# One kilobyte a partition of a weight load sent as a transfer whose source has an outer dimension of 4

## The chip, the cores and the metric

The kernel runs on one core of a Trainium2 chip. The metric is the device time of one execution in microseconds; the median of three runs is 216.96 us (216.91 to 217.72). One execution was taken with the hardware profiler, and all rows shown are from that one. Its data comes from HBM through 16 DMA engines, which work side by side. A transfer is cut into packets, each a contiguous run of bytes, and the packets are shared out among the engines; a transfer has landed when the last engine that carries a part of it is done.

## The reference

A decode step for two sequences: a layer norm of one token each, a window attention over the last 4096 cached positions, a gated MLP, and the product of both added to the input.

```python
def _A_ref(x, k_cache, v_cache, wq, wo):
    B, Sq, D = x.shape                       # 2, 1, 512
    Hq, Dh = 32, 128
    Hkv, Sk = k_cache.shape[1], k_cache.shape[2]   # 8, 32768
    W = min(4096, max(256, Sk // 4))         # 4096
    rep = Hq // Hkv
    q = (x @ wq).reshape(B, Sq, Hq, Dh).transpose(0, 2, 1, 3)
    k = jnp.repeat(k_cache[:, :, Sk - W:, :], rep, axis=1)
    v = jnp.repeat(v_cache[:, :, Sk - W:, :], rep, axis=1)
    scores = jnp.einsum("bhqd,bhkd->bhqk", q, k) * (Dh ** -0.5)
    p = _softmax(scores, axis=-1)
    o = jnp.einsum("bhqk,bhkd->bhqd", p, v)
    return o.transpose(0, 2, 1, 3).reshape(B, Sq, Hq * Dh) @ wo

def _B_ref(x, w_in, w_sp, b_sp, w_out):
    z = _gelu(x @ w_in)                      # F = 1792, Fh = 896
    z1, z2 = z[..., :Fh], _layernorm(z[..., Fh:], axis=-1)
    g = jnp.einsum("ts,bsf->btf", w_sp, z2) + b_sp[None, :, None]
    return (z1 * g) @ w_out

xn = _layernorm(A_x)
return A_x + _A_ref(xn, ...) * _silu(_B_ref(xn, ...))
```

## The kernel before

All is float32. The input is 89.4 MB, nearly all of it the two caches' windows (16 loads of 4 MB, named k and v in the profile), wq (8 MB), wo (8 MB), w_in (3.5 MB) and w_out (1.75 MB). Every large load is issued on SP's queue, in program order, and each is spread over all 128 partitions.

**Buffers.** `slot` gives out 4 buffers of 32 KB a partition, in turn: w_in, wq rows for k = 0 and 1, wq rows for k = 2 and 3, K0, K1, V0, K2, V1 and so on. A load into a buffer is issued once the work that reads the buffer's earlier content is done. So K1 waits for the w_in products, V0 for the first half of wq, K2 for the second half, and later loads for the transposes (K) or the products (V) of the unit three loads back.

**wq.** Its row number is 4p + k (p the partition, k = 0 to 3), so a partition holds four neighbouring rows of 16 KB. The first two come in one transfer of 4 MB (line 130, a = 0), the other two in one transfer of 2 MB each (a = 2). `queries(k)` (lines 262 to 269) multiplies row group k: 8 products of 32 columns of `xnT[:, k, :]` (the normed input, transposed, with its 512 elements split in the same way) with 512 columns of wq, summed over k in two PSUM banks `pq`. The profile names them `q_ps`; each shows as two MATMUL entries. Between them lie the norm of the MLP's second half and, behind them, `y` (w_out), the copies `qs`, the transposes `qx`, the masked copies `xm`, the product `qa`, and `place_queries` (line 337), which fills `qb`.

**xnT.** Lines 193 to 198: the normed input `xn` is transposed by four TensorE transposes (one for each k) into PSUM and copied to `xnT`, whose unused columns were cleared.

**Attention.** Eight units of two heads each run through a hand-written order (the table ORDER, lines 27 to 52): transposes of K on VectorE (`T`, tile kts), shares and scores on TensorE, the softmax on ScalarE, products with V (`pv`, tile acc).

**The end.** wo comes in 4 MB, then pieces of 2, 1, 0.5, 0.25 and 0.25 MB (`load_wo`, lines 511 to 518), the last ones so that the last products (`Z`, tile so) have little left to do when the last bytes land. After `Z:3` come two VectorE operations (`res`) and the store.

**Small loads.** Line 139 loads x into `x4` with a source of outer dimension 4 (`by_group`, line 138: 4 x 2 x 128 elements), on ScalarE's queue, beside the first large load.

Of the kernel before, what the change touches and what calls it, by code (L numbers as in the profile page):

```python
# [9 lines left out]
F32 = mybir.dt.float32  # L10
# [4 lines left out]
P = 128  # L15
HQ, DH = 32, 128
# [4 lines left out]
def free_ap(t, offset, dims):  # L21

    return bass.AP(tensor=t.tensor, offset=t.offset + offset, ap=[list(t.ap[0])] + [list(d) for d in dims])
# [47 lines left out]
def kernel(  # L71
# [14 lines left out]
    pe, dve, act, sp = (InOrder(tc, e) for e in (nc.tensor, nc.vector, nc.scalar, nc.sync))  # L86
    B, _, D = x.shape
# [7 lines left out]
    KT = D // P  # L95
# [3 lines left out]
    DC = D // G  # L99
    SCALE = DH ** -0.5  # L100
    OFF = 30000.0 / SCALE

    fit = ctx.enter_context(tc.tile_pool(name="fit", bufs=1))
    fit.tile([P, 480], F32, tag="fit", name="fit")
# [2 lines left out]
    cst = ctx.enter_context(tc.tile_pool(name="cst", bufs=1))  # L107
# [3 lines left out]
    def slot(name, *shape):  # L111
        return ring.tile([P, *shape], F32, tag="slot", name=name)

    def bank(name, *shape):
        return ps.tile([P, *shape], F32, tag="kt", name=name, bufs=2)
# [9 lines left out]
    wq_v = wq.rearrange("(p k) f -> p k f", p=P)  # L125
    wqt = []
    for a in range(0, KT, 2):
        t = slot(f"wq{a}", 2, HQ * DH)
        for k, n in ((0, 2),) if a == 0 else ((0, 1), (1, 1)):
            sp.dma_start(t[:, k : k + n], wq_v[:, a + k : a + k + n, :])  # L130
        wqt += [t[:, 0], t[:, 1]]

    wb1 = cst.tile([1, 2], F32, tag="wb1", name="wb1")
# [21 lines left out]
    ident = cst.tile([P, P], F32, tag="ident", name="ident")  # L155
    make_identity(nc, ident)
    selw = cst.tile([P, 60], F32, tag="selw", name="selw")
    nc.gpsimd.memset(selw, 0.0)
    xnT = cst.tile([P, KT, 32], F32, tag="xnT", name="xnT")
    nc.gpsimd.memset(xnT, 0.0)  # L160
    ones = cst.tile([P, P], F32, tag="ones", name="ones")
    nc.gpsimd.memset(ones, 1.0)
# [29 lines left out]
    rsqrt(rs, va, "x")  # L192
    xn = sb.tile([B, D], F32, tag="o", name="xn", bufs=1)
    dve.tensor_scalar(xn, xs, mv[:, 0:1], rs, op0=ALU.subtract, op1=ALU.mult)
    pt = bank("xnT_ps", KT, B)
    for k in range(KT):
        pe.transpose(pt[:, k, :], xn.rearrange("b (p k) -> b k p", k=KT)[:, k, :], ident[:B, :B])
    dve.tensor_copy(xnT[:, :, :B], pt)

    same = cst.tile([P, G, 32], F32, tag="same", name="same")  # L200
# [15 lines left out]
    dve.tensor_reduce(other, free_ap(rowm, 0, [[4, 2], [8, REP]]), axis=AX.X, op=ALU.add)  # L216
    dve.tensor_scalar(other, other, -OFF, OFF, op0=ALU.mult, op1=ALU.add)
    diag = cst.tile([P, 4], F32, tag="diag", name="diag")
# [18 lines left out]
    for n in range(G):  # L237
        pz = bank(f"z{n}", 512)[:, :FC]
        for k in range(KT):
            pe.matmul(  # L240
                pz[32 * k : 32 * k + 32, :], xnT[:, k, :], win[:, k, n * FC : (n + 1) * FC],
                start=True, stop=True,
# [9 lines left out]
    pt = bank("zT_ps", 2, FT, B)  # L252
# [7 lines left out]
    pq = [ps.tile([P, 512], F32, tag=f"s{r}", name=f"q_ps{r}") for r in range(NR)]  # L260

    def queries(k):
        for r in range(NR):
            for g in range(G):
                c = (r * G + g) * 512
                pe.matmul(
                    pq[r][32 * g : 32 * g + 32, :], xnT[:, k, :], wqt[k][:, c : c + 512],
                    start=(k == 0), stop=(k == KT - 1),
                )

    queries(0)
    zT = cst.tile([P, 2, FT, B], F32, tag="zT", name="zT")
    dve.tensor_copy(zT, pt)
# [19 lines left out]
    per_b = [[0, FT], [1, B]]  # L293
    mean_over_rows(mean, z2, "mean_ps")
    queries(1)
    dve.tensor_scalar_mul(mean, mean, 1.0 / FH)
    dve.tensor_sub(z2, z2, free_ap(mean, 0, per_b))
# [5 lines left out]
    dve.tensor_scalar(z2, z2, wb[:, 0:1], wb[:, 1:2], op0=ALU.mult, op1=ALU.add)  # L303
    dve.tensor_mul(hT[:, :, 0 : 16 * B : 16], z1, z2)
    queries(2)
    queries(3)

# [4 lines left out]
    for j in range(FT):  # L312
        for g in range(G):
            pe.matmul(
                y[32 * g : 32 * g + 32, :], hT[:, j, :], wout[:, j, g * DC : (g + 1) * DC],
                start=(j == 0), stop=(j == FT - 1),
# [277 lines left out]
    for u in range(NU):  # L594
        p = Unit()
        p.u, p.m, p.kt, p.sh, p.ss, p.s, p.p, p.pT = u, None, {}, {}, {}, {}, {}, {}
        units.append(p)
    for line in ORDER.strip().split("\n"):
        for name in line.split():
            name, at = name.split(":")  # L600
            u, _, a = at.partition(".")
# [34 lines left out]
```

## Time and profile before

| what | value |
|---|---|
| median of 3 runs | 216.96 us (216.91 to 217.72) |
| profiled execution: its own time | 217.3 us |
| profiled execution: span, first to last instruction | 215.4 us |
| TensorE busy, share of the span | 65% |
| VectorE busy | 58% |
| ScalarE busy | 24% |
| read from HBM | 89.40 MB, 415 GB/s over the span |

An engine's share of busy time is an average over the whole span. The DMA row of the page counts how busy the 16 DMA engines are on average, so a share of 0.50 can mean that eight of them are busy and eight are done. Instruction rows give start, duration and, in brackets, how long the engine stood idle before and what released it. DMA rows on SPq are the issuing of a transfer, not its movement.

### The profile page before, as it was taken

The page shows a single profiled execution, that of the slowest core. Times are in us where ns is not written, and L with a number is a line of the kernel's source. Part 1 is how long each engine was busy: PE and PEld are TensorE (multiplying, and loading weights), DVE is VectorE, ACT ScalarE, POOL GpSimd, SP SyncE. Part 2 cuts the span into 40 slices and gives each one's busy share as a digit, 9 for nine tenths or more (in the row PEclk, how much of TensorE's full clock was granted, in tenths as well). Part 3 has the DMA queues.
Part 4 walks back from the last instruction along what each step waited for, and adds up shares of the span by engine and source line. Part 5 has one row for each costly group of instructions (what it writes and reads, how often), then busy time and mean ns, then how long its engine had stood idle before and what let it go on. Part 6 is the DMA issues. An engine that isn't in the chain of part 4 may idle for free.

```text
span 215.4 us, 2476 instructions
## 1 busy us (share of the span) xinstructions
PE 139.0 (65%) x972; PEld 50.7 (24%) x972; DVE 125.7 (58%) x217; ACT 51.1 (24%) x128; POOL 5.2 (2%) x19
## 2 busy tenths in 40 slices
PE   0179594503857985934890796289359628988893
PEld 0118431300111222302230231113113211243242
DVE  2511212349799899639927981994698099535001
ACT  5010203200116036122330503151251306152210
POOL 8000000000000000000000000000000000000000
PEclk9999589955785799995899599559859985997999
DMA  7999999999999999999999999999999999999990
GB/s 256 427 438 456 396 435 456 408 458 408 463 414 441 426 426 444 417 458 408 450 420 444 423 420 450 426 450 417 438 415 444 432 420 456 405 463 402 414 377 29
DMA packets 3930, 89.54 MB, mean 416 GB/s; under 512 B 446, under 2 KB 462, under 8 KB 848
## 3 DMA queue, kind: packets, MB, share of 16 engines
q1 hardware_dynamic: 3900, 89.40, 96.8%
q8 instruction: 7, 0.11, 0.2%
q14 instruction: 3, 0.02, 0.0%
q10 hardware_dynamic: 20, 0.01, 0.0%
HBM read 89.40 MB, written 0.00 MB: 415 GB/s over the span
## 4 chain that ended last, share of the span: by engine, by line
DMA 68%; DVE 23%; ACT 3%; PE 2%; issue 1%; SPq 1%
DMA k<-in_A_k_cache_dram 51%; DVE kts L65 18%; DMA wo<-in_A_wo_dram 12%; DMA win<-in_B_w_in_dram 5%; DVE pT L65 2%; ACT p L65 2%; PE sh L65 2%; DVE m L65 1%; DVE gate L65 1%; SPq L65 1%; DVE nb L65 1%; PE s L65 1%; DVE qb L65 1%; ACT ss L65 0%; DVE res L65 0%
## 5 line engine op out<-in xcount | busy, mean ns | idle before, releaser
L65 DVE STREAM_TRANSPOSE kts<-k 128x1024 f32<-128x1024 f32 x64 | 75.6, 1218 | 31.2 <-DMA k<-in_A_k_cache_dram 31.2
L65 PE MATMUL sh<-kts,qb 128*32 128x512 f32 x256 | 43.4, 803 | 15.5 <-DVE kts L65 12.0
L65 PE MATMUL acc<-v,pT 128*32 128x512 f32 x256 | 35.1, 665 | 6.5 <-DMA v<-in_A_v_cache_dram 4.3
L65 ACT ACTIVATE p<-s,nb 128x512 f32<-128x512 f32 x32 | 22.5, 730 | 38.8 <-DVE nb L65 38.8
L65 ACT ACTIVATE ss<-sh 128x512 f32<-128x512 f32 x16 | 9.6, 598 | 62.0 <-PE sh L65 62.0
L65 PE MATMUL mo<-mg,joint 128*128 128x16 f32 x16 | 4.2, 342 | 26.0 <-DVE mg L65 26.0
L65 DVE STREAM_TRANSPOSE pT<-p 128x1024 f32<-128x1024 f32 x16 | 19.6, 1225 | 2.3 <-ACT p L65 2.1
L65 PE MATMUL s<-ss,sums 128*128 128x512 f32 x32 | 17.9, 642 | 2.5 <-ACT ss L65 2.5
L65 PEld LDWEIGHTS sh<-kts,qb 128*32 128x32 f32 x256 | 9.1, 129 | 37.3 <-issue 33.4
L65 PEld LDWEIGHTS acc<-v,pT 128*32 128x32 f32 x256 | 10.6, 142 | 30.9 <-issue 21.7
L65 DVE TENSOR_REDUCE m<-s 128x1 f32<-128x512 f32 x16 | 10.8, 673 | 4.8 <-PE s L65 4.8
L65 ACT ACTIVATE o<-acc,wd 128x128 f32<-128x128 f32 x32 | 9.1, 368 | 15.3 <-PE acc L65 15.3
L65 PE MATMUL q_ps<-wq,xnT 128*32 128x512 f32 x64 | 9.0, 689 | 5.2 <-DMA wq<-in_A_wq_dram 5.2
L65 PEld LDWEIGHTS mo<-mg,joint 128*128 128x128 f32 x16 | 3.4, 263 | 29.8 <-DVE mg L65 26.9
L65 PE MATMUL z<-win,xnT 128*32 128x448 f32 x32 | 4.9, 742 | 4.5 <-DMA win<-in_B_w_in_dram 4.5
L65 PEld LDWEIGHTS s<-ss,sums 128*128 128x128 f32 x32 | 4.9, 191 | 11.0 <-issue 8.2
L65 PE MATMUL part<-wo,oT 128*32 128x512 f32 x48 | 6.2, 595 | 1.0 <-DMA wo<-in_A_wo_dram 1.0
L65 PE MATMUL zT_ps<-rowm,z 128*128 128x2 f32 x28 | 6.6, 370 | 0.0
L65 PEld LDWEIGHTS zT_ps<-rowm,z 128*128 128x128 f32 x28 | 6.5, 325 | 0.0
L65 ACT ACTIVATION_READ_ACCUMULATOR p<-s,nb 128x1 f32 x32 | 6.3, 197 | 0.0
L65 ACT ACT_TABLE_LOAD x4 | 5.1, 1283 | 2.6 <-POOL hT L164 2.6
L65 DVE TENSOR_REDUCE o<-col 128x32 f32<-128x128 f32 x6 | 1.6, 270 | 6.9 <-PE col L65 6.9
(108 smaller groups left out, 70.3 us busy)
## 6 DMA issues: line engine op xcount, KB each, us to landing
k<-in_A_k_cache_dram SPq DMA_DIRECT2D x8, 4096.0 KB, 26.8
v<-in_A_v_cache_dram SPq DMA_DIRECT2D x8, 4096.0 KB, 31.7
wq<-in_A_wq_dram SPq DMA_DIRECT2D x1, 4096.0 KB, 24.4
wq<-in_A_wq_dram SPq DMA_DIRECT2D x2, 2048.0 KB
wo<-in_A_wo_dram SPq DMA_DIRECT2D x1, 4096.0 KB, 31.8
win<-in_B_w_in_dram SPq DMA_DIRECT2D x1, 3584.0 KB, 11.3
wo<-in_A_wo_dram SPq DMA_DIRECT2D x1, 2048.0 KB
wout<-in_B_w_out_dram SPq DMA_DIRECT2D x1, 1792.0 KB, 15.1
```

What stands on the lines that cost most here:

```text
L65: return self.tc.keep_in_program_order(call(*args, **kwargs))
```

## The change

The second half of wq (row groups k = 2 and 3, 32 KB a partition) was loaded in two transfers of 16 KB a partition. Now one transfer carries all of it but the last 1 KB of each partition (31 KB, contiguous), and a second one carries that last 1 KB: 256 columns, the end of row group 3. The second one's source is written as 4 x 32 x 256 with the strides of one, four and no partitions: source partition c + 4d goes to partition 32c + d. So in these 256 columns the rows lie in another order among the partitions. The normed input is therefore transposed a fifth time in that order (`xnl`, a reordering copy on VectorE, one more TensorE transpose, and a fifth row group in `xnT`), and the last of the 8 products of `queries(3)` is split into two of 256 columns, the second with the reordered `xnT`.

```diff
+    LAST, FEW = 256, 4
...
-        for k, n in ((0, 2),) if a == 0 else ((0, 1), (1, 1)):
-            sp.dma_start(t[:, k : k + n], wq_v[:, a + k : a + k + n, :])
+        if a == 0:
+            sp.dma_start(t, wq_v[:, a : a + 2, :])
+        else:
+
+            of, to = wq_v[:, a : a + 2, :].rearrange("p k f -> p (k f)"), t.rearrange("p k f -> p (k f)")
+            n, at = 2 * HQ * DH - LAST, wq.offset + KT * HQ * DH - LAST
+            sp.dma_start(to[:, :n], of[:, :n])
+            few = [[KT * HQ * DH, FEW], [FEW * KT * HQ * DH, P // FEW], [1, LAST]]
+            sp.dma_start(to[:, n:], bass.AP(tensor=wq.tensor, offset=at, ap=few))
...
-    xnT = cst.tile([P, KT, 32], F32, tag="xnT", name="xnT")
+    xnT = cst.tile([P, KT + 1, 32], F32, tag="xnT", name="xnT")
...
-    pt = bank("xnT_ps", KT, B)
+    xnl = cst.tile([B, FEW, P // FEW], F32, tag="xnl", name="xnl")
+    dve.tensor_copy(xnl, xn.rearrange("b (d c k) -> b c d k", c=FEW, k=KT)[:, :, :, KT - 1])
+    pt = bank("xnT_ps", KT + 1, B)
     for k in range(KT):
         pe.transpose(pt[:, k, :], xn.rearrange("b (p k) -> b k p", k=KT)[:, k, :], ident[:B, :B])
+    pe.transpose(pt[:, KT, :], xnl.rearrange("b c d -> b (c d)"), ident[:B, :B])
...
-                pe.matmul(
-                    pq[r][32 * g : 32 * g + 32, :], xnT[:, k, :], wqt[k][:, c : c + 512],
-                    start=(k == 0), stop=(k == KT - 1),
-                )
+                n = 512 - LAST if k == KT - 1 and c + 512 == HQ * DH else 512
+                for rows, i, j in ((k, 0, n), (KT, n, 512)):
+                    if i < j:
+                        pe.matmul(
+                            pq[r][32 * g : 32 * g + 32, i:j], xnT[:, rows, :], wqt[k][:, c + i : c + j],
+                            start=(k == 0), stop=(k == KT - 1 and j == 512),
+                        )
```

## The prediction

> **What bounds the kernel now.** First the page's slices, queues and chain, to see what is full.
>
> ```profile
> DMA  7999999999999999999999999999999999999990
> ...
> q1 hardware_dynamic: 3900, 89.40, 96.8%
> q8 instruction: 7, 0.11, 0.2%
> q14 instruction: 3, 0.02, 0.0%
> q10 hardware_dynamic: 20, 0.01, 0.0%
> ...
> DMA 68%; DVE 23%; ACT 3%; PE 2%; issue 1%; SPq 1%
> ...
> k<-in_A_k_cache_dram SPq DMA_DIRECT2D x8, 4096.0 KB, 26.8
> ```
>
> The DMA engines are full in 38 of 40 slices. The VectorE share in the chain is deceptive: the chain follows what released each issue, but a K load of 4.19 MB needs 9.7 us at the rate below and lands 26.8 us after its issue, so in the middle it stands some 17 us behind other transfers. A delayed issue costs nothing until that is used up.
>
> Next the stretches, coarse in the middle and fine at the end; the last two columns are DMA share and GB/s.
>
> ```profile
> 60.00:200.00 140.00, 97.40 (x606) 31.36 (x610) 100.23 (x145) 39.78 (x108) 0.00 (x0) 0.82 1.00 433
> ...
> 209.75:210.00 0.25, 0.25 (x20) 0.25 (x15) 0.00 (x0) 0.16 (x1) 0.00 (x0) 1.00 0.55 213
> 210.00:210.25 0.25, 0.25 (x15) 0.10 (x4) 0.00 (x0) 0.00 (x0) 0.00 (x0) 1.00 0.51 197
> 210.25:210.50 0.25, 0.20 (x10) 0.08 (x8) 0.00 (x0) 0.00 (x0) 0.00 (x0) 1.00 0.50 197
> 210.50:210.75 0.25, 0.25 (x12) 0.25 (x16) 0.00 (x0) 0.00 (x0) 0.00 (x0) 1.00 0.31 115
> 210.75:211.00 0.25, 0.25 (x18) 0.25 (x12) 0.00 (x0) 0.00 (x0) 0.00 (x0) 1.00 0.09 33
> 211.00:211.25 0.25, 0.25 (x20) 0.23 (x11) 0.00 (x0) 0.00 (x0) 0.00 (x0) 1.00 0.07 25
> 211.25:211.50 0.25, 0.25 (x12) 0.00 (x0) 0.00 (x0) 0.00 (x0) 0.00 (x0) 1.00 0.00 0
> ```
>
> For 140 us all 16 engines run without a gap, at 433/16 = 27.1 GB/s each. But they don't finish together: at 210.25 half of them (0.50 x 16) still move data, from 210.75 on about one. So the end is set not by the bytes over 16 engines but by the one engine that is last. Then the chain's last pieces:
>
> ```profile
> 185.48 26.11 DMA wo<-in_A_wo_dram
> 211.59 0.04 issue
> 211.64 0.47 PE so L65 x8
> 212.11 0.02 issue
> 212.13 0.30 DVE res L65
> ```
>
> The last wo piece lands at 211.59, 0.34 us after its last packet, and TensorE takes it up at once. What the last engine gains or loses goes into the time one for one.
>
> **Which engine is late, and why.** The groups don't tell engines apart, but the trace has every packet's start, length and size. On one engine the packets follow each other without a gap, so each chain can be followed by its phase: the lag of its last packet of a transfer behind the earliest engine's. Worked out from these records:
>
> ```
> lag in ns after w_in | after the last cache load | end of the chain, us
>   *115 |  670 | 209.60      341 | 1756 | 210.69
>   *155 | 1575 | 210.51      445 | 1859 | 210.79
>   *193 | 1872 | 210.81      492 | 1912 | 210.85
>   *349 |  349 | 209.28      890 |  890 | 211.24
> others end between 208.93 and 210.56
> packets of 512 bytes on queue q10 (the load of x4): 6.66 and 7.74, 6.74 and 7.82, 6.89 and 7.98, 9.90 and 10.98
> ```
>
> Lags stay the same to a few ns from transfer to transfer, except where one of the ten instruction packets of q8 and q14 starts at a chain's packet boundary. A q8 packet (16 KB) puts that chain back by about 1.4 us, a q14 packet (8 KB) by 0.6 to 0.8. The chain at 890 is struck at 205.1 us, put back 1.42 us, and ends last, 0.39 us after the next. Chain 193 was struck twice by q14.
>
> The stars mark the four chains in which x4's 512-byte packets stand, two each. That load is the one whose source also has an outer dimension of 4, so it shows where the new transfer will go: onto chains 115, 155, 193 and 349 alone.
>
> **The change part by part.**
>
> *31 KB in one transfer.* In the records the two 2 MB transfers of wq take 9.725 us on each engine, a 4 MB transfer of 32 KB packets 9.681. Taking 8 x 1 KB away at 27.1 GB/s is 0.303, so the new transfer takes 9.378. **All 16 chains gain 0.347 us.**
>
> *1 KB packets on four chains.* 128 packets are 32 for each. A packet of 1 KB that streams isn't in the trace. From below: 1024 bytes at 27.1 GB/s, 37.8 ns. From above: the price of a 2 KB packet, where the row of 209.75 gives 213/0.55/16 = 24.2 GB/s, so 85 ns. I take 42 ns: the end's packets (8, 4 and 2 KB) fit bytes at that rate plus 4.7 ns each, and 512 bytes alone take 27. So 32 x 42.3 + 6 for the semaphore = 1.36 us (1.22 to 2.73). **The four chains net +1.01 us** (+0.87 to +2.38), the other twelve -0.35.
>
> *The end.* Chain 890 goes from 211.24 to 210.89, chain 492 to 210.50. Chain 193 goes from 210.81 to **211.82**, chain 155 to 211.52. The last is now chain 193, at 211.82 - 211.24 = **+0.58 us** (+0.44 to +1.95).
>
> The Trainium skill (DMA: Bandwidth & Descriptors, Rules for kernel authors, "Use all 16 engines") speaks against the edit: an outermost dimension c below 16 confines a transfer to c engines. The x4 packets agree. Taken by itself that rule prices the transfer at four times its time on 16 engines, +1.0 us on those four; it says nothing of which engine ends last.
>
> *The work around it.* The extra copy on VectorE, the fifth transpose and its wider copy lie ahead of w_in:
>
> ```profile
> 6.99 0.55 PEld L65 LDWEIGHTS xnT_ps<-ident,xn 2*128 2x128 f32 x4 [6.99 <-issue]
> 7.66 0.17 DVE L65 COPY xnT<-xnT_ps 128x8 f32<-128x8 f32 x1 [0.79 <-PE xnT_ps L65]
> 7.74 0.22 DVE L65 COPY same<-rowm 128x128 f32<-128x128 f32 x1
> 12.16 2.47 PE L65 MATMUL z<-win,xnT 128*32 128x448 f32 x12 [4.54 <-DMA win<-in_B_w_in_dram]
> ```
>
> They cost at most 0.22 + 0.55/4 + some ns, and TensorE waits 4.54 us for w_in behind them: nothing. VectorE's later set-up copies move by as much and end before 12 too. The split product adds one entry pair and no columns.
>
> More moves in `queries(2)`: its rows now land with group 3's.
>
> ```profile
> 31.73 1.92 PE L65 MATMUL q_ps<-wq,xnT 128*32 128x512 f32 x16
> 36.62 1.92 PE L65 MATMUL q_ps<-wq,xnT 128*32 128x512 f32 x16 [2.97 <-DMA wq<-in_A_wq_dram]
> 38.60 0.53 SPq L65 DMA_DIRECT2D k<-in_A_k_cache_dram  x1
> 42.33 1.14 PE L65 MATMUL qa<-xm,same 128*128 128x256 f32 x2 [2.26 <-DVE xm L65]
> 46.27 1.25 DVE L65 STREAM_TRANSPOSE kts<-k 128x1024 f32<-128x1024 f32 x1 [4.09 <-DMA k<-in_A_k_cache_dram]
> 47.44 1.18 DVE L65 TENSOR_TENSOR qb<-qa,grpm 128x1024 f32<-128x1024 f32 x1
> 75.26 3.50 DVE L65 STREAM_TRANSPOSE kts<-k 128x1024 f32<-128x1024 f32 x3 [0.34 <-DMA k<-in_A_k_cache_dram]
> ```
>
> `queries(2)` waits until about 36, so both groups run from there: 1.92 us later for y, qs, qx, xm and qa, which ended at 43.47 and now at about 45.5 to 46. VectorE stands 4.09 us before K0's transposes, so qx and xm fit, and `qb` needs qa only at 47.44. If the cover failed, VectorE would be up to a microsecond late at K0. Behind the longer queries, SP waits with K2 (38.60, then about 40.5) and everything queued after it; K2 lands near 75, 36 us after issue for 9.7 us of transfer, so some 26 us cover it. SP issues the same number of transfers. Cost: nothing.
>
> **Sum.** The profiled execution took 217.3, its span 215.4. With +0.58 the span would be 216.0. The median of the runs shown is 0.34 below the profiled time; against it the forecast is 216.96 + 0.58 = **217.5 us**.
>
> **The rivals.**
>
> 1. *The four engines and the others crowd where they write* (slower). Now a 1 KB piece from partition group 32c to 32c + 31 is written by one engine, into partitions that several engines fill at full rate at that moment. If the 27.1 GB/s is a limit of the destination and not of the engine, each 1 KB packet shares it with a full stream and takes twice 42, 85 ns: the upper bound, chain 193 at 210.81 - 0.35 + 2.73 = 213.19, +1.95 us, 218.9. It decides the sign at 0.5% from 59 ns a packet on. For it: all engines run at one and the same rate, as at a common wall. Against it: x4's 512-byte packets took 27 ns beside running streams, and the streams' packets didn't grow; but these are only 512 bytes each. The Trainium skill (DMA: Bandwidth & Descriptors, Where 436 GB/s comes from) puts the wall at the memory's ports, 435 GB/s for 16; the 433 of the row is near it, and no row tells port from engine. Chance 0.27.
>
> 2. *The late chains are others in the timed executions* (a little faster). Which chain an instruction packet strikes decides who is last. If chains 193 and 155 are not struck, the four end at their 349 or 670 lags plus 1.01, all under 210.7, and the time moves with the twelve: -0.35, 216.6; with the last packet striking elsewhere as well it could be -0.75, 216.2. For it: lags come from ten packets only, and the median is 0.34 below the profile. Against: the strikes follow instruction counts, which hardly change. Chance 0.18.
>
> 3. *The transfer goes over all 16 engines after all*, its 128 destination partitions deciding. Then each carries 8 packets, 8 x 42 = 0.34, against -0.35: no change, 217.0. x4 speaks against it. Chance 0.05.
>
> **How the numbers follow.** Forecast 0.50, rivals 0.27, 0.18, 0.05. About what a measurement of this kernel can tell from no change is 0.5%, 1.08 us: 215.9 to 218.0. The forecast, rivals 2 and 3 lie inside, rival 1 mostly beyond (its milder prices, under 59 ns, not). From the forecast's own tail some 0.06 goes past 218.0 by strikes on a loaded chain; of rival 2, 0.06 goes to luck beyond -0.5%. Faster 0.06, within 0.62, slower 0.32. The range is 216.4 (rival 2) to 219.0 (rival 1); the forecast's own is 217.3 to 218.0.
>
> **What would show it.** Right: 128 packets more of 1 KB and 256 fewer of 16 KB; four chains behind by about 1.0 us from 36 us on, the others earlier by 0.35; at the end a lone engine until about 211.8. Wrong: 1 KB packets of 60 ns or more, or streams that lengthen beside them (rival 1); a last chain without 1 KB packets (rival 2); 16 chains with 1 KB packets (rival 3); a DMA share under 1.00 in the middle, which would mean that a late K2 was not covered.

## The result and the profile after

The changed kernel takes 218.45 us (median of 12 runs, 218.01 to 220.87) against 217.01 (12 runs, 216.87 to 218.06): a ratio of 1.0069, with a 95% interval from 1.0044 to 1.0095. It is slower by 1.4 us. The profiled execution took 218.42, its span is 216.5 where before had 215.4.

First the packet line and queue q1 of the page, before and after. Its counts are of packets smaller than 512 bytes, 2 KB and 8 KB, each including the ones before.

```profile
DMA packets 3930, 89.54 MB, mean 416 GB/s; under 512 B 446, under 2 KB 462, under 8 KB 848
```

```profile
DMA packets 3918, 89.54 MB, mean 414 GB/s; under 512 B 434, under 2 KB 578, under 8 KB 964
## 3 DMA queue, kind: packets, MB, share of 16 engines
q1 hardware_dynamic: 3888, 89.40, 96.5%
q8 instruction: 7, 0.11, 0.2%
q14 instruction: 3, 0.02, 0.0%
```

Between 512 bytes and 2 KB there were 16 packets and now are 144: the 128 packets of 1 KB. Below 512 there are 12 fewer, the packets that signal an engine's share as done: the small transfer has 4 of them and not 16, so it did go over four engines. The bytes are the same.

The stretches of the changed kernel, columns as in the prediction (stretch and its length, then busy time and number of instructions of PE, PEld, DVE, ACT and POOL, TensorE's granted clock, DMA share, GB/s):

```profile
60.00:200.00 140.00, 95.78 (x607) 29.79 (x598) 101.14 (x143) 39.95 (x108) 0.00 (x0) 0.84 1.00 432
...
210.50:210.75 0.25, 0.25 (x11) 0.25 (x12) 0.00 (x0) 0.00 (x0) 0.00 (x0) 1.00 0.63 246
210.75:211.00 0.25, 0.25 (x18) 0.25 (x13) 0.00 (x0) 0.07 (x1) 0.00 (x0) 1.00 0.32 123
211.00:211.25 0.25, 0.25 (x19) 0.25 (x13) 0.00 (x0) 0.25 (x1) 0.00 (x0) 1.00 0.23 90
211.25:211.50 0.25, 0.25 (x15) 0.19 (x5) 0.00 (x0) 0.25 (x1) 0.00 (x0) 1.00 0.07 25
...
212.25:212.50 0.25, 0.25 (x16) 0.15 (x8) 0.00 (x0) 0.00 (x0) 0.00 (x0) 1.00 0.06 25
212.50:212.75 0.25, 0.17 (x8) 0.00 (x0) 0.00 (x0) 0.00 (x0) 0.00 (x0) 1.00 0.00 0
```

The middle is as full as before. At the end one engine (0.06 to 0.07 x 16) is alone from about 211.3 to 212.5; before, the lone engine was done by 211.25. The chain says the same, landing at 212.82 instead of 211.59:

```profile
187.17 25.65 DMA wo<-in_A_wo_dram
212.82 0.04 issue
212.86 0.47 PE so L65 x8
```

So the time was lost on one DMA engine. Where on its way, the packet records tell. The following is worked out from them: the lag behind the earliest engine of the four chains with 1 KB packets, and when the earliest engine itself passed that point (us from the span's start).

```
                              earliest   lags of the four chains, ns
after the first wq transfer    24.834    104  204  231  337
after the 31 KB transfer       34.214    104  204  231  337
after the 1 KB transfer                  1736 1826 1868 2040   (against 34.214)
after K0                       44.439    1515 1568 1607 1707
after the last cache load     189.662    3308 2130 1601 1701
end of the last chain         212.507
packets of K0 (32 KB) that took over 1.216 us: 30, 7.95 us over 1.213 in sum;
  the longest 1.911 (its engine struck by an instruction packet), the others up to 1.752
packets of 1 KB: 128, median 0.046 us, mean 0.055, nine in ten up to 0.068, one 0.361
```

The 31 KB transfer took 34.214 - 24.834 = 9.380 us on the earliest engine, as forecast (9.378). Then K0 took 10.225 us on it and not 9.681: even an engine that carries no 1 KB packet lost 0.54 us. In the profile of before every 32 KB packet of K0 at this place took 1.213 us. So the streams were lengthened beside the small transfer, and the four chains were set back by more than their own packets' time.

The work around it, in the order of time in the changed kernel:

```profile
6.88 0.26 DVE L65 COPY xnl<-xn 2x128 f32<-2x128 f32 x1
7.47 0.24 PE L65 MATMUL xnT_ps<-ident,xnl 2*128 2x2 f32 x1
12.04 1.72 PE L65 MATMUL z<-win,xnT 128*32 128x448 f32 x8 [4.33 <-DMA win<-in_B_w_in_dram]
...
36.55 5.34 PE L65 MATMUL q_ps<-wq,xnT 128*32 128x512 f32 x34 [4.40 <-DMA wq<-in_A_wq_dram]
41.99 0.54 SPq L65 DMA_DIRECT2D k<-in_A_k_cache_dram  x1
45.67 1.12 PE L65 MATMUL qa<-xm,same 128*128 128x256 f32 x2 [2.25 <-DVE xm L65]
46.61 1.25 DVE L65 STREAM_TRANSPOSE kts<-k 128x1024 f32<-128x1024 f32 x1 [1.08 <-DMA k<-in_A_k_cache_dram]
47.78 1.19 DVE L65 TENSOR_TENSOR qb<-qa,grpm 128x1024 f32<-128x1024 f32 x1
```

The additions ahead of w_in cost nothing: TensorE waits 4.33 us behind them. The queries start at 36.55 and take 5.34 us, not 3.84. The granted clock explains the difference, in the stretches from there on (the third number from the end is the clock's share):

```profile
36.50:37.00 0.50, 0.45 (x4) 0.19 (x8) 0.00 (x0) 0.00 (x0) 0.00 (x0) 0.62 0.49 197
37.00:38.00 1.00, 1.00 (x8) 0.21 (x4) 0.00 (x0) 0.00 (x0) 0.00 (x0) 0.50 1.21 524
```

TensorE, idle for 4.40 us before, is granted half its clock here. `qa` ends at 46.79, and VectorE's idle time before K0 shrinks from 4.09 to 1.08 us, but `qb` still follows the first transpose without a gap. The cover held, narrowly.

### The profile page after: what moved, and what is told of

Same layout as the page of the kernel before. It is cut to its first block, busy times and chain, and to the rows that moved or that the text cites. A ratio compares the mean times of both kernels' runs of the same rounds, so it can differ in the third digit from the quotient of the medians.

```text
span 216.5 us, 2483 instructions
## 1 busy us (share of the span) xinstructions
PE 141.3 (65%) x975; PEld 51.3 (24%) x975; DVE 126.0 (58%) x218; ACT 51.0 (24%) x128; POOL 5.2 (2%) x19
## 4 chain that ended last, share of the span: by engine, by line
DMA 68%; DVE 22%; PE 5%; ACT 3%; issue 1%; SPq 1%; ACTq 0%
DMA k<-in_A_k_cache_dram 51%; DVE kts L65 16%; DMA wo<-in_A_wo_dram 12%; DMA win<-in_B_w_in_dram 5%; PE sh L65 3%; DVE pT L65 2%; ACT p L65 2%; PE s L65 1%; DVE m L65 1%; DVE gate L65 1%; SPq L65 1%; DVE nb L65 1%; ACT ss L65 1%; DVE qb L65 1%; DVE res L65 0%
## 5 line engine op out<-in xcount | busy, mean ns | idle before, releaser
L65 PE MATMUL sh<-kts,qb 128*32 128x512 f32 x256 | 42.9, 795 | 12.7 <-DVE kts L65 9.1
L65 PE MATMUL s<-ss,sums 128*128 128x512 f32 x32 | 18.8, 672 | 2.5 <-ACT ss L65 2.5
L65 PE MATMUL q_ps<-wq,xnT 128*32 128x512 f32 (+1 forms) x66 | 10.9, 809 | 6.1 <-DMA wq<-in_A_wq_dram 6.1
L65 DVE STREAM_TRANSPOSE qx<-qs 128x512 f32<-128x512 f32 x2 | 1.3, 690 | 7.7 <-PE y L65 7.7
```

Of the source, the lines that this page charges most:

```text
L65: return self.tc.keep_in_program_order(call(*args, **kwargs))
```

## The experiments

**Theory A:** four engines carry 32 packets more each and crowd with the others where they write; the end goes to the loaded engine that is late already. **Rivals:** B, 1 KB packets as such disturb the streams; C, the cost lies in the two row groups landing together or in the extra products; D, the crowding arises in the reading, not in the writing. Medians and ratios are against the kernel before on the same chip; its median was 217.22 beside the first four runs, 217.05 beside the next four, and 217.23 (one run) beside the last two.

**The 1 KB transfer over 16 engines (e1_sixteen).**

```diff
-        for k, n in ((0, 2),) if a == 0 else ((0, 1), (1, 1)):
-            sp.dma_start(t[:, k : k + n], wq_v[:, a + k : a + k + n, :])
+        of, to = wq_v[:, a : a + 2, :].rearrange("p k f -> p (k f)"), t.rearrange("p k f -> p (k f)")
+        n = 2 * HQ * DH - (256 if a else 0)
+        sp.dma_start(to[:, :n], of[:, :n])
+        if a:
+            sp.dma_start(to[:, n:], of[:, n:])
```

> The same cut, 31 KB and 1 KB a partition, but the 1 KB transfer in the partitions' own order (outer dimension 128), so that all 16 engines carry 8 of its packets each, and the products as before. Theory A (the four engines carry 32 packets each, and crowd with the others where they write): each chain -0.35 + 8 x 0.042, nothing left to see: within 0.3 us of before, and the first packets of K0 keep their 1.213 us. Rival B (1 KB packets read at a pitch of 64 KB disturb the running streams, whoever carries them): K0's first packets lengthen by about 0.5 us as in the changed kernel, time +0.5 us or more. Rival C (the cost comes from row groups 2 and 3 landing together, late queries and a late K2): about +1.2 us, as in the changed kernel.

217.27 us, ratio 0.9998 (0.9987 to 1.0010). All 128 packets of 1 KB took 0.046 us, and of K0's packets here one alone was longer by more than 0.01 us, by 0.47, beside an instruction packet on its engine. That speaks against B: the same 128 pieces cost nothing when each engine carries eight of them, and 70 of them started while K0's packets ran. The order of reading is another one, though: in the changed kernel an engine steps over four partitions from piece to piece. e5_own below keeps that order and lengthens nothing either, and with it B falls. C falls here for the row groups, since both land together.

**One transfer of 4 MB (e2_merged).**

```diff
-        for k, n in ((0, 2),) if a == 0 else ((0, 1), (1, 1)):
+        for k, n in ((0, 2),):
```

> The second half of wq in one transfer of 4 MB, no small transfer, products as before. Theory A: -0.05 us (8 packets of 32 KB cost 9.681 us on an engine, 16 of 16 KB 9.725): no change to be seen. Rival C: row groups 2 and 3 land together here too, so most of the +1.4 us should come: +0.8 us or more.

217.24 us, ratio 1.0007 (0.9992 to 1.0022). The queries at half clock are here as well, and VectorE has 0.51 us left before K0:

```profile
36.76 5.34 PE L65 MATMUL q_ps<-wq,xnT 128*32 128x512 f32 x32 [4.21 <-DMA wq<-in_A_wq_dram]
45.88 1.12 PE L65 MATMUL qa<-xm,same 128*128 128x256 f32 x2 [2.26 <-DVE xm L65]
46.25 1.25 DVE L65 STREAM_TRANSPOSE kts<-k 128x1024 f32<-128x1024 f32 x1 [0.51 <-DMA k<-in_A_k_cache_dram]
```

So the late queries and the late K2 are hidden here, as the prediction had it.

**The extra products alone (e7_products):** the transfers of before, with the copy, the fifth transpose and the split product.

```diff
+    xnl = cst.tile([B, FEW, P // FEW], F32, tag="xnl", name="xnl")
+    dve.tensor_copy(xnl, xn.rearrange("b (d c k) -> b c d k", c=FEW, k=KT)[:, :, :, KT - 1])
...
+                for rows, i, j in ((k, 0, n), (k, n, 512)):
```

> The transfers of the kernel before with the changed kernel's extra work on the engines: the reordering copy, the fifth transpose, the wider copy and the split product (both halves in the old order of rows). Theory A: hidden, within 0.2 us of before. Rival C (the products and copies cost the time): +0.5 us or more.

217.11 us, ratio 0.9995 (0.9975 to 1.0015): nothing. What is left of the change is the transfer over four engines.

**Twice as much on four engines (e3_double).**

```diff
-    LAST, FEW = 256, 4
+    LAST, FEW = 512, 4
```

> 2 KB a partition instead of 1 KB on four engines. Theory A: 32 packets of 0.080 us instead of 0.042 put 1.2 us more on the four chains, the main transfer is 0.3 us shorter, and the crowding lasts twice as long (0.5 to 1.0 us more): 1.4 to 2.0 us above the changed kernel, 219.8 to 220.5. If the excess over the packets' own time is a fixed price of such a transfer: 0.9 us above it, 219.3. Rival C: no more than the changed kernel, 218.4.

220.20 us (220.10 to 220.21), ratio 1.0135 (1.0121 to 1.0150): within what theory A gave, not a fixed price. The 2 KB packets of this transfer took 0.131 us in the middle; at the end of the same run 2 KB packets take 0.084. K0's packets were longer by 20.6 us in sum, against 7.95 with 1 KB: the crowding grows faster than the bytes.

**Eight engines (e4_eight, e9_eight_look, e10_eight_look).**

```diff
-    LAST, FEW = 256, 4
+    LAST, FEW = 256, 8
```

> The same kernel with an outer dimension of 8 instead of 4: eight engines with 16 packets each. Theory A: the chain that ends last gets 16 x 0.042 = 0.68 us instead of 1.36 and half the crowding of its own packets: 0.2 to 0.6 us above before, 217.2 to 217.6. Rival C: as the changed kernel, 218.4.

The seven runs fell in two groups: 217.42 to 218.74 (four, with spans of 215.5 to 215.9) and 219.55 to 219.98 (three, 217.1 to 217.6). The median 218.74 and the ratio 1.0063 (1.0027 to 1.0098) mix them, and lie above what was expected. The profiled one is of the shorter group: K0's packets longer by 3.9 us in sum, half of what four engines cause. Of the shorter group two times lie within the expected 217.2 to 217.6, and all its spans are 0.2 to 0.6 us above 215.3, the median span of the kernel before beside them, where four engines give +1.1. So in this group it counts how much each engine carries; the longer group ended later than the changed kernel's median, and nothing here explains it. Two more runs were to find what makes a run long.

> The kernel with eight engines once more, since its runs fell in two groups, spans of 215.5 to 215.9 and of 217.1 to 217.6 us. Theory A: in a long run an instruction packet strikes one of the eight loaded chains (1.4 us) that it misses in a short one; the end is then one lone chain for 1.4 to 2 us, with K0's packets lengthened as in the short run (3 to 4 us in sum). If instead the crowding itself varies, the sum of K0's lengthened packets differs between short and long runs by several us.

> As the run before it: the same kernel, one more look, to have a long and a short run side by side.

Both were short (217.32 and 217.28, spans of 215.5; K0's packets longer by 4.6 and 4.1 us). No long run was profiled, so its cause stays open. In e10_eight_look most of the queries ran at half clock, and the cover was used up, though by so little that the time doesn't show it:

```profile
36.51 6.32 PE L65 MATMUL q_ps<-wq,xnT 128*32 128x512 f32 x34 [3.44 <-DMA wq<-in_A_wq_dram]
47.78 1.22 DVE L65 TENSOR_TENSOR qb<-qa,grpm 128x1024 f32<-128x1024 f32 x1 [0.16 <-PE qa L65]
```

**Own partitions or others' (e5_own, e6_cross).** Both load 64 KB that nothing reads, on top of all that the kernel before loads.

```diff
+    few = bass.AP(tensor=wq.tensor, offset=wq.offset + KT * HQ * DH - 256, ap=[[KT * HQ * DH, 4], [4 * KT * HQ * DH, 16], [1, 256]])
+    sp.dma_start(wide[0:16, 7168:8192].rearrange("p (j f) -> p j f", j=4), few)     # e5_own
+    sp.dma_start(wide[0:64, 7168:7424], few)                                        # e6_cross
```

`wide` is w_in's buffer, taken in its full 32 KB a partition; the kernel's own loads are those of before.

> The kernel before (both 2 MB transfers) with 64 KB more, which nothing reads: a transfer with an outer dimension of 4, 16 packets of 1 KB on each of four engines, read at the same pitch of rows as in the changed kernel and placed behind wq, ahead of K0. Its target is the unused end of w_in's buffer in partitions 0 to 15, four neighbouring partitions an engine. By the Trainium skill (DMA: Bandwidth & Descriptors, The descriptor swizzle) these are the partitions that those engines write in every large transfer. Theory A with the crowding at the destination: K0's packets keep 1.213 us (one struck by an instruction packet aside), the four chains get 16 x 0.042 = 0.68 us, and the time is 0.2 to 0.4 us above before. Rival D (the crowding comes from reading 1 KB pieces at that pitch, on the HBM side): K0's first packets lengthen on all engines, half as much as in the changed kernel, some 3 to 4 us in sum, wherever the target lies.

> The same 64 KB, source, packets and place in the queue as the run before it, but to partitions 0 to 63, 256 columns each, 16 partitions an engine: so the four engines write partitions that other engines fill. Theory A with the crowding at the destination: K0's first packets lengthen, by 1.5 us or more in sum, on about half of the chains (those that write partitions 0 to 63), the rest keep 1.213; the time is 0.4 to 0.8 us above before. Rival D: as in the run before it, no difference between the two.

e5_own took 217.67 us, ratio 1.0024 (1.0003 to 1.0046); e6_cross 217.79, ratio 1.0029 (1.0013 to 1.0046). The intervals overlap, so the times alone don't part them. The packet records do:

```
             1 KB packets: median, longest   K0's longer packets: number, sum   last packet ends
e5_own           0.046   0.046 us             1   0.46 us                        211.55
e6_cross         0.046   0.146 us            16   1.37 us                        211.83
before                                        0                                  211.25
```

In e5_own the one longer packet stands beside an instruction packet; in e6_cross such a packet accounts for 0.54 us of the sum. The source and the 16 packets on each of four engines are the same in both; only the target differs. Where each engine writes four neighbouring partitions, no stream notices, though all 64 small packets start while K0's run. Where each writes sixteen partitions, fifteen more of K0's packets lengthen, by 0.83 us in sum. So the target matters, and D falls.

What was expected of e6_cross did not come as a whole. The fifteen packets stand on all eleven engines that carried no small packet and were not struck, ten of them with their first packet of K0; expected were about half of the chains, those that fill partitions 0 to 63, and 1.213 us for the rest. So the crowding is not confined to the streams into the partitions that are written, and what the streams share stays open. Nor do the two targets differ in one thing alone: e5_own puts four pieces side by side into each of 16 partitions, e6_cross one piece into each of 64, and no run sent the pieces into 16 partitions of other engines. The crowding was also smaller than I had put down (0.83 us, not 1.5 or more).

The price of the small packets themselves is not settled either. e5_own's median is 0.62 us above before, where 0.2 to 0.4 was expected; e6_cross's 0.74 lies in its 0.4 to 0.8. Against the profile of before the ends come 0.30 and 0.58 us later, and from the 0.68 us alone +0.25 would follow; but the span of that profile is 215.4, and beside these runs the kernel before has a median span of 215.0. Against that, the median spans of 215.75 and 215.9 are 0.75 and 0.9 longer. The tails show the order of the two, e5_own first:

```profile
211.00:211.25 0.25, 0.25 (x20) 0.20 (x8) 0.00 (x0) 0.00 (x0) 0.00 (x0) 1.00 0.06 25
211.25:211.50 0.25, 0.25 (x17) 0.17 (x8) 0.00 (x0) 0.00 (x0) 0.00 (x0) 1.00 0.06 25
211.50:211.75 0.25, 0.19 (x8) 0.00 (x0) 0.00 (x0) 0.00 (x0) 0.00 (x0) 1.00 0.00 0
```

and e6_cross, whose lone engine runs a stretch longer:

```profile
211.25:211.50 0.25, 0.25 (x20) 0.24 (x11) 0.00 (x0) 0.00 (x0) 0.00 (x0) 1.00 0.06 25
211.50:211.75 0.25, 0.25 (x20) 0.17 (x8) 0.00 (x0) 0.00 (x0) 0.00 (x0) 1.00 0.08 33
211.75:212.00 0.25, 0.23 (x10) 0.00 (x0) 0.00 (x0) 0.00 (x0) 0.00 (x0) 1.00 0.00 0
```

The Trainium skill (DMA: Bandwidth & Descriptors, The descriptor swizzle) names partitions 0 to 3, 4 to 7, 8 to 11 and 12 to 15 as among those that engines 0 to 3 write in a 128-partition transfer, and e5_own, built on that, agrees as far as it lengthened no stream. The records hold no engine numbers, so no run here shows which four engines carried the pieces.

**The changed kernel once more (e8_after).**

> The changed kernel once more, beside the runs of this call on one chip. Theory A: +1.2 to +1.5 us over before, K0's first packets lengthened by 7 to 8 us in sum on all engines, the last chain one that carries 1 KB packets and was struck twice by 8 KB instruction packets.

218.29 us, ratio 1.0058 (1.0040 to 1.0076). K0's packets were longer by 8.5 us in sum (7 to 8 expected). In the packet records the last chain is again one of those with 1 KB packets, and was struck twice by 8 KB instruction packets (its lag was 2.63 us after the first strike and 3.48 after the second). The clock was full here, the queries took 3.65 us and VectorE idled 4.64 us before K0:

```profile
35.65 3.65 PE L65 MATMUL q_ps<-wq,xnT 128*32 128x512 f32 x34 [3.08 <-DMA wq<-in_A_wq_dram]
43.08 1.12 PE L65 MATMUL qa<-xm,same 128*128 128x256 f32 x2 [2.26 <-DVE xm L65]
47.57 1.25 DVE L65 STREAM_TRANSPOSE kts<-k 128x1024 f32<-128x1024 f32 x1 [4.64 <-DMA k<-in_A_k_cache_dram]
```

and yet the kernel was as slow: the half clock is not what costs the time.

No version is measurably faster than the kernel before. The merged load saves too little to be measured, and the transfer over a few engines costs more than the 0.35 us that it takes from the others.

## Why the prediction came out as it did

The time lies in the stated range (216.4 to 219.0), but above the forecast's own (217.3 to 218.0), and the rise of 0.69% is past the 0.5% that I gave 0.32; that no difference would be told had 0.62. What sets the end was right: one engine, loaded and struck. One term of the sum was too small, because it left the crowding out. That the time still lies in the range is owed to rival 1, whose price set the upper bound, and not to the forecast's own terms. By the prediction's own list, the packets and the lone engine came as for "right" (the engine until 212.5, not 211.8), the lengthened streams as for "wrong".

- *The end belongs to one engine, a loaded one that instruction packets had put back.* Right. The last chain carried 1 KB packets and had been struck twice by 8 KB instruction packets, in both profiles of the changed kernel.
- *"All 16 chains gain 0.347 us."* Right for the transfer itself (9.380 us on the earliest engine). But in K0 that engine lost 0.54 us again, so after K0 the earliest engine was about 0.2 us later and not 0.35 earlier.
- *"32 x 42.3 + 6 for the semaphore = 1.36 us."* This is the step that was mis-sized. From the records the four chains' lags grew from 104, 204, 231 and 337 to 1515, 1568, 1607 and 1707, 1.38 us in the mean, and the earliest engine had lost 0.54 itself: 1.92 us, which is 60 ns for each of the 32 packets instead of 42. About 0.29 of the missing 0.56 us lies in the small transfer (1.65 us in the mean), the rest in their first K0 packet. The bounds, 1.22 to 2.73, held it. With 1.92 in place of 1.36 the sum becomes +1.14 us, against +1.1 in the span and +1.23 in the last landing.
- *Rival 1, the crowding.* Given 0.27 as an alternative, it came true in part beside the forecast: streams lengthened. That they do so because the target is shared, as rival 1 has it, is not shown; in e6_cross streams lengthened that were expected not to. My argument against it, that x4's 512-byte packets took 27 ns and lengthened no stream, was too weak: 4 KB in all passed unnoticed where 128 KB did not. I had also looked for its price in the 1 KB packets; most of them kept 46 ns (0.055 us in the mean), and the streams beside them paid. It was to decide the sign at 59 ns a packet (58, redone from the same terms); 60 came.
- *Rival 2, other late chains.* Not seen in the profiles: in both of the changed kernel one loaded chain was struck twice by 8 KB instruction packets and ended last, as chain 193 was struck before. The timed executions without a profile can't tell.
- *Rival 3, all 16 engines.* Wrong, by the 12 fewer signalling packets; e1_sixteen shows what it would have given.
- *The stars.* One of the four was misplaced. x4's packets at 9.90 and 10.98 us stand in the chain with lag 175 after w_in (181 later), not 155. It doesn't enter the sum, since chain 193 was last anyway.
- *"Cost: nothing" for queries, K2, copies and products.* Right (e2_merged, e7_products). But I had counted the queries at full clock; at half clock `qa` ended at 46.79 and not at 45.5 to 46, and of 4.09 us of cover 1.08 was left. With eight engines it was once used up (e10_eight_look).

The medians rose by 1.44 us, the profiled spans by 1.1, and in e8_after the median by 1.24 and the median span by 1.35. These differences lie within the intervals.

## What to carry to other kernels

Where transfers keep all DMA engines full, the end is set by the engine that is last, not by the mean: follow the packets' chains before moving bytes among engines, and ask which engine is late and what strikes it. A transfer over few engines was paid for twice here, by the packets that those engines carried and by the streams beside them; only with four neighbouring partitions for each engine (e5_own) did the streams keep their pace. The second part (0.54 us on the earliest engine) was larger than the 0.35 us taken off the others, and it showed in the records as longer packets of the neighbours more than of the transfer itself.

## What the runs showed of the hardware

- Four engines writing 128 KB in 1 KB pieces across all partitions lengthened the 32 KB packets behind and beside them from 1.213 to as much as 1.752 us (1.813 in e8_after), 7.95 and 8.5 us in sum, one packet struck by an instruction packet included; eight engines 3.9 to 4.6; 256 KB in 2 KB pieces on four engines 20.6. Sixteen engines with eight packets each caused none, nor did four engines with 64 KB in partitions 0 to 15, four neighbouring ones each. The same 64 KB over partitions 0 to 63 lengthened packets on all eleven unloaded, unstruck engines, by 0.83 us in sum.
- An instruction packet of 16 KB puts the engine that it lands on back by about 1.4 us, one of 8 KB by 0.6 to 1.0. Ten such packets, unequally spread, and the lags of up to 0.89 us that were there after w_in left the engines ending up to 2.3 us apart in the kernel before (208.93 to 211.24).
- TensorE's granted clock after an idle stretch differed between runs of nearly the same work: half after 4.40 us in the changed kernel's first profile, full after 3.08 us in its second, and half after 2.32 us in e1_sixteen. So the length of the idle stretch alone does not tell it.
